# An S4D convolution beside a GLU: spectra at 2048 quarter-shifted frequencies instead of 2049 whole ones

## The chip, the cores and the metric

The kernel runs on one core of one Trainium2 chip. The metric is device time in microseconds (us) of one execution. Engines are named as in the profile: PE (TensorE matmul) and PEld (its weight loads), DVE (VectorE), ACT (ScalarE), POOL (GpSimd), and SP, which here only issues DMAs. SP, ACT and POOL each have a DMA queue; an instruction that waits in such a queue holds all that is behind it on the same engine.

## What is computed

A token sequence of 2048 x 448 is layer-normed, and two branches read the result: an S4D convolution and a gated linear unit (GLU). Cut to what matters:

```python
def _A_ref(u, log_A_real, A_imag, C_real, C_imag, log_dt, D_skip):   # L = 2048, D = 448, N = 256
    dt = exp(log_dt); A = -exp(log_A_real) + 1j * A_imag; C = (C_real + 1j * C_imag) * dt[:, None]
    P = exp((A * dt[:, None])[:, :, None] * arange(L)[None, None, :])
    K = 2.0 * einsum("dn,dnl->dl", C, P).real
    y = irfft(rfft(u_t, 2 * L) * rfft(K, 2 * L), 2 * L)[:, :, :L]     # causal convolution
    return y + u * D_skip
def _B_ref(x, w_gate, w_up, w_down):                                  # F = 1792
    return (sigmoid(x @ w_gate) * (x @ w_up)) @ w_down
xn = layernorm(A_u)
return A_u + _A_ref(xn, ...) + _B_ref(xn, ...)
```

## The kernel before

Two Python generators write the program: `conv()` (norm, the kernel K, the spectra) and `glu()`. A planner loop at the end of the kernel function takes the next piece from the generator whose planned share done, `done[i] / total[i]`, is smaller; a piece tells its planned cost when it yields. `total[0]` is the sum of the convolution's planned costs, its last term `17 * WS` with `WS = 4.5`. The tile framework then orders each engine's instructions, with priorities (`hp`) and `issue_after` hints, and each engine runs its list in order. When the GLU comes to its last output tiles it yields `None`, and the convolution is written out to its end before the GLU goes on.

**The kernel stage** (`kgen`): for 56 chunks of 8 channels, DVE makes three products (`Et` twice, lines 591 and 592, `Ft`, line 593) from magnitudes (POOL) and phases (ACT), and PE multiplies them (`ko`, line 605). Every fourth chunk ACT copies `ko` to `ks` (line 618), and the first stage of the kernel's transform (`kp`, `kq`, line 555) writes a bank of the kernel's half-done spectra to DRAM (`sk_d`, 14 banks). GLU pieces lie in between: gate and up matmuls (`gu`, line 697, 11 per weight half), `hf` and `hl` on DVE (708, 715), the down projection (`po`, line 808).

**The spectra stage** (`spectra`): the convolution is done as a transform of 64 x 64 points. `x1_d` holds the first stage of x's transform, `sk_d` that of the kernel's. The channels are in two halves `h` of 224. A step `(h, k)` treats four first-stage frequencies `k` to `k + 3`:

- `loads` issues, on SP, two DMAs of x (`sx`), one of the tables (`tb`), one of the kernel (`skl`), three steps ahead (`NLD = 3`).
- `there` is the second stage for both on PE (`sp`, line 890: 32 matmul records of 128 x 64), a copy of the kernel's spectra by ACT (`kc`, line 898), and the complex product on DVE (lines 901 to 904).
- `back` is the first stage of the way back on PE (`pv`, line 917: 16 records), two ACT copies to `vt` (line 923), and four stores to `v_d` (line 935). It is called in the next step.
- `turned` loads a step's rows of `v_d` into `vp`, a tile with one buffer (line 941). It is called one step after `back`.
- `last(h, m)` is the last stage: 32 products `pv<-vp,wf` (line 952), added to the accumulators by DVE (line 960). After its first two calls for the first half, `out` stores finished tokens through the SP, ACT and POOL queues in turn (line 237).

With whole frequencies 0 to 2048, first-stage frequencies 0 and 32 are each real in part: frequencies 0 to 31 are packed in eight steps for each half, and frequency 32 gets a step of its own for both halves, `(None, 32)`, second of 17. That step uses 64 rows, its own tables `t32`, and the kernel rows of all 14 banks. `last` for the first half runs in the steps `due[0]` and `due[0] + 1`; `due` is set when `turned(0, 28)` is called:

```python
steps[0:2] = [steps[1], (None, 32), steps[0]]
...
if t == (0, 28):
    due = [n + 1]
```

The second half's `turned` calls wait until that last stage is through, since `vp` has one buffer. The last stage of the second half is written by `glu()`, after the final down projections.

Of the kernel before, what the change touches and what calls it, by code (L numbers as in the profile page):

```python
# [11 lines left out]
F32 = mybir.dt.float32  # L12
# [10 lines left out]
F = 1792  # L23
NA = 32
NB = 64
NK1 = 33
TWO_PI = 2.0 * math.pi
MAGIC = 1.5 * 2.0**23
NFT = F // 128
# [26 lines left out]
def _tables():  # L56

    a = np.arange(NA)[:, None]
    k1 = np.arange(NK1)[None, :]
    ang = 2 * np.pi * ((a * k1) % 64) / 64.0  # L60


    wk = np.zeros((4, NA, 2, 2, 32))

    wx = np.zeros((4, NA, 64))
    for j in range(4):
        wk[j, :, 0, j % 2] = np.cos(ang)[:, :32]
        wk[j, :, 1, j % 2] = -np.sin(ang)[:, :32]
        wk[j, :, 1, j % 2, 0] = np.cos(ang)[:, 32]
        wx[j, :, :NK1] = np.cos(ang)  # L70
        wx[j, :, NK1:] = -np.sin(ang)[:, 1:32]
    b = np.arange(NB)[:, None]
    k2 = np.arange(64)[None, :]
    tab = np.zeros((NK1, 128, 128))
    bk = np.zeros((2, 2, 64, 2, 128))
    for q in range(NK1):
        al = 2 * np.pi * ((b * (q + 64 * k2)) % 4096) / 4096.0
        c, s = np.cos(al), np.sin(al)
        tab[q] = np.block([[c, -s], [s, c]])
        if q in (0, 32):  # L80


            for h in range(2):

                split = lambda t: t.reshape(64, 2, 32).transpose(0, 2, 1)
                both = lambda r, i: np.stack([split(r), split(i)], 3).reshape(64, 128)
                bk[q // 32, h, :, 0] = both(c.T, s.T)
                bk[q // 32, h, :, 1] = both(-s.T, c.T)

    tab[0, 64:] = 0.0  # L90
    t32 = np.concatenate([tab[32][:, None], bk[1].reshape(128, 2, 128)], 1)
    tab = tab[:32].reshape(8, 4, 128, 128).transpose(0, 2, 1, 3)

    wf = np.zeros((2, 2, 4, 8, 32, NA))
    for k in range(32):
        ang = 2 * np.pi * ((k * (64 * np.arange(NA)[None] + np.arange(64)[:, None])) % 4096) / 4096.0
        re = (1.0 if k == 0 else 2.0) / 4096.0 * np.cos(ang)
        im = -2.0 / 4096.0 * np.sin(ang)
        if k == 0:
            im = np.broadcast_to(np.cos(np.pi * np.arange(NA))[None] / 4096.0, im.shape)  # L100
        wf[:, 0, k % 4, k // 4] = re.reshape(2, 32, NA)
        wf[:, 1, k % 4, k // 4] = im.reshape(2, 32, NA)
# [13 lines left out]
    return {  # L116
        "c_wk": f(wk, (128, 2, 64)),
        "c_wx": f(wx, (128, 64)),
        "c_tab": f(tab, (8, 128, 4, 128)),
        "c_t32": f(t32, (128, 3, 128)),  # L120
        "c_bk": f(bk[0], (128, 2, 128)),
        "c_wf": f(wf, (128, 32, NA)),
        "c_sel": f(sel, (128, 512)),
        "c_id": np.eye(128, dtype=np.float32),
    }
# [3 lines left out]
def s4d_glu_kernel(ctx, tc, io):  # L129
# [700 lines left out]
    def spectra(pf):  # L830
# [19 lines left out]
        def loads(h, k):  # L850
            sx = pf.tile([128, 4, H], F32, name="sx", bufs=NLD)
            sk = pf.tile([128, 7, 4, 32], F32, name="skl", bufs=NLD)
            if k == 32:

                nc.sync.dma_start(sx[:64, 0:2].rearrange("b h d -> b (h d)"), x1_d[32])
                for i in range(2):
                    nc.sync.dma_start(sk[:64, :, i], sk_d[64:, 7 * i : 7 * i + 7, 0])
                return t32, sk, sx
            ds, gs = slice(H * h, H * h + H), slice(7 * h, 7 * h + 7)
            nc.sync.dma_start(sx[0:64], x1_d[k : k + 4, :, ds].rearrange("k b d -> b k d"))  # L860
# [10 lines left out]
        def after():  # L871
            return tc.issue_after(sp_mm[0].ins)

        def there(k, tb, sk, sx):

            kk, np_ = (64, 64) if k == 32 else (128, 128)
            ys_ = []
            for j in range(2):

                ks = [(0, j, 0)] if k == 32 else [(2 * j + i, 2 * j + i, i) for i in range(2)]  # L880
                pss = []
                for src in (sk, sx):
                    ps = bank("sp")
                    with after():
                        for c in range(2):
                            for t, n, i in ks:
                                to, rhs = ps[64 * i : 64 * i + 64, c], sx[:kk, n]
                                if src is sk:
                                    to, rhs = to.rearrange("p (g d) -> p g d", d=32), sk[:kk, :, n]
                                mm = nc.tensor.matmul(  # L890
                                    to, tb[:kk, t, 64 * c : 64 * c + 64], rhs, start=True, stop=True,
                                    skip_group_check=True,
                                )
                    sp_mm[:] = [mm]
                    pss.append(ps)
                    if src is sk:
                        kc = work("kc", [128, 2, H], 3)
                        nc.scalar.copy(kc[:np_], ps[:np_])
                yy, pd = work("yy", [128, 2, H], 4), work("pd", [128, 2, H], 2)
                xt = pss[1]  # L900
                v.tensor_tensor(yy[:np_], kc[:np_], xt[:np_], ALU.mult)
                v.tensor_tensor(pd[:np_], kc[:np_], xt[:np_, ::-1], ALU.mult)
                v.tensor_tensor(yy[:np_, 0], yy[:np_, 0], yy[:np_, 1], ALU.subtract)
                v.tensor_tensor(yy[:np_, 1], pd[:np_, 0], pd[:np_, 1], ALU.add)
                ys_.append(yy)
            return ys_

        def back(h, k, ys_):
            vt = work("vt", [128, 2, 2, H], 2)
            bt, n = (t32[:, 1:3], 1) if k == 32 else (bk, 2)  # L910
            pvs = [bank("pv") for _ in range(n)]
            with after():
                for j in range(2):
                    for e in range(2):
                        for i in range(n):
                            s = slice(64 * i, 64 * i + 64)
                            mm = nc.tensor.matmul(  # L917
                                pvs[i][:, j], bt[s, e], ys_[j][s, e], start=(e == 0), stop=(e == 1),
                                skip_group_check=True,
                            )  # L920
            sp_mm[:] = [mm]
            for i in range(n):
                nc.scalar.copy(vt[:, i], pvs[i])


            for j in range(2):
                for i in range(n):
# [48 lines left out]
        for n, (h, k) in enumerate(steps):  # L976

            sp_mm[:] = glu_mm
            if prev is not None:
                back(*prev)  # L980
            cur = there(k, *ld[n])
            if n + NLD < len(steps):
                ld.append(loads(*steps[n + NLD]))
            if 4 <= n < 8:
# [159 lines left out]
```

## Time and profile before

| | us |
|---|---|
| three timed runs | 740.15, 739.62, 736.60 (median 739.62) |
| the profiled execution | 742.26, span 740.5 |
| PE busy | 683.2 (92% of the span) |
| DVE, ACT, POOL busy | 562.3, 421.7, 376.8 |
| mean granted TensorE clock | 0.967 of full speed |
| kernel stage: first and last `kp` products | about 178 to 552 |
| spectra stage: first `sp` to last `pv` of `back` | 557.6 to 717 |

Rows of the profile read: start, duration, engine, line, operation, output <- inputs, count, and in brackets how long the engine was idle before and what released it. Groups give total busy time, mean ns of one, the idle time before, and its releasers. In the chain, a row is a stretch of the path that ended last. Matmuls overlap, so their single durations add up to more than their stretch; the chain's stretches don't overlap. A record count for fp32 matmuls is twice that of the matmuls in the code.

### The profile page before, as it was taken

How to read it: one execution, taken by the hardware profiler on the slowest of the kernel's cores; microseconds unless marked ns; L12 is line 12 of the kernel's file. 1: busy time of each engine (PE TensorE's matmuls, PEld its weight loads, DVE VectorE, ACT ScalarE, POOL GpSimd, SP SyncE). 2: the span in 40 equal slices, each digit the busy share in tenths (PEclk: the TensorE clock that was granted, in tenths of full speed). 3: DMA queues.
4: the chain of work that ended last, by engine and by line, in shares of the span. 5: the costliest groups of instructions: out<-in, count | busy, mean ns of one | idle time of the engine just before them, and what ended most of it. 6: DMA issues, size and time to landing. Idle time of an engine off the chain costs nothing.

```text
span 740.5 us, 19082 instructions
## 1 busy us (share of the span) xinstructions
PE 683.2 (92%) x7780; PEld 537.0 (73%) x7780; DVE 562.3 (76%) x776; ACT 421.7 (57%) x650; POOL 376.8 (51%) x423
## 2 busy tenths in 40 slices
PE   2797899997999999889989999999999999998994
PEld 1675688785887787556767887888877777776783
DVE  5679997699889989878569978987865555554553
ACT  3535445667688877887567867866742222322310
POOL 2111018697678987964538685796855002341001
PEclk9898899997999999979999999999999999999997
DMA  9936428524413452625852243232169999999646
GB/s 207 219 84 182 119 79 245 173 88 160 165 50 108 163 191 80 183 82 151 267 190 91 79 131 114 96 104 70 59 154 282 255 245 239 234 242 258 173 132 163
DMA packets 93287, 116.76 MB, mean 158 GB/s; under 512 B 12176, under 2 KB 81168, under 8 KB 92944
## 3 DMA queue, kind: packets, MB, share of 16 engines
q1 hardware_dynamic: 83888, 95.08, 46.4%
q10 hardware_dynamic: 6736, 14.57, 6.2%
q0 software_dynamic: 2576, 5.90, 3.2%
q8 instruction: 61, 1.00, 0.6%
q14 instruction: 26, 0.21, 0.1%
HBM read 70.75 MB, written 44.76 MB: 156 GB/s over the span
## 4 chain that ended last, share of the span: by engine, by line
PE 56%; DVE 11%; POOL 9%; ACT 7%; DMA 7%; issue 4%; SPq 3%; ACTq 1%; POOLq 0%; DVEq 0%
PE gu L697 21%; PE po L808 14%; PE sp L890 7%; PE ko L605 5%; PE pv L917 4%; POOL me L507 4%; PE tr L529 3%; POOL mf L507 3%; DVE Ft L593 1%; DVE Et L591 1%; POOL dl L778 1%; ACT S L540 1%; DMA acc_d<-acc 1%; DVE Et L592 1%; DVE wl L752 1%
## 5 line engine op out<-in xcount | busy, mean ns | idle before, releaser
L507 POOL TENSOR_TENSOR me<-me,pm 128x32 f32<-128x32 f32 (+1 forms) x168 | 143.2, 852 | 87.8 <-DVE Et L592 76.0
L507 POOL TENSOR_TENSOR mf<-mf,pm 128x64 f32<-128x64 f32 (+1 forms) x112 | 123.0, 1099 | 4.2
L697 PE MATMUL gu<-xh,wh 128*128 128x512 f32 x336 | 101.8, 409 | 4.2 <-ACT xh L218 4.2
L591 DVE TENSOR_TENSOR Et<-me,S 128x1024 f32<-128x1024 f32 x56 | 84.6, 1511 | 17.2 <-ACT S L540 15.9
L697 PE MATMUL gu<-xh,wl 128*128 128x512 f32 x336 | 96.9, 396 | 0.0
L697 PE MATMUL gu<-xl,wh 128*128 128x512 f32 x336 | 96.7, 393 | 0.0
L808 PE MATMUL po<-dh,hh 128*128 128x448 f32 x224 | 86.3, 385 | 5.2 <-DVE acc L813 2.5
L592 DVE TENSOR_TENSOR Et<-me,S 128x1024 f32<-128x1024 f32 x56 | 78.7, 1405 | 10.8 <-ACT me L520 10.3
L808 PE MATMUL po<-dl,hh 128*128 128x448 f32 x224 | 84.2, 376 | 1.1 <-POOL dl L778 1.1
L808 PE MATMUL po<-dh,hl 128*128 128x448 f32 x224 | 83.1, 373 | 0.0
L593 DVE TENSOR_TENSOR Ft<-mf,S 128x1024 f32<-128x1024 f32 x56 | 78.5, 1402 | 6.0 <-POOL mf L507 3.1
L537 ACT ACTIVATE S<-tr 128x1024 f32<-128x1024 f32 x56 | 57.6, 1029 | 41.0 <-PE tr L529 38.3
L697 PEld LDWEIGHTS gu<-xh,wh 128*128 128x128 f32 x336 | 62.2, 192 | 23.4 <-ACT xh L218 5.8
L713 ACT CAST hh<-hf 128x512 fp32r<-128x512 f32 x56 | 35.0, 625 | 74.8 <-DVE hf L708 58.4
L605 PEld LDWEIGHTS ko<-Et,Ft 128*32 128x32 f32 x3584 | 55.0, 111 | 30.6 <-issue 11.9
L697 PEld LDWEIGHTS gu<-xh,wl 128*128 128x128 f32 x336 | 64.4, 192 | 15.5 <-DVE pl L306 0.7
L605 PE MATMUL ko<-Et,Ft 128*32 128x64 f32 x3584 | 65.7, 224 | 10.7 <-DVE Ft L593 7.6
L697 PEld LDWEIGHTS gu<-xl,wh 128*128 128x128 f32 x336 | 63.5, 189 | 14.2 <-issue 0.7
L708 DVE SCALAR_TENSOR_TENSOR hf<-th,gu 128x512 f32<-128x512 f32 x56 | 38.2, 682 | 37.1 <-PE gu L697 28.3
L540 ACT ACTIVATE S<-S,hpi 128x1024 f32<-128x1024 f32 x56 | 65.5, 1170 | 0.0
L813 DVE SCALAR_TENSOR_TENSOR acc<-po,acc 128x448 f32<-128x448 f32 x80 | 48.3, 616 | 20.6 <-PE po L808 20.5
L715 DVE TENSOR_TENSOR hl<-hf,hh 128x512 fp32r<-128x512 f32 x56 | 47.6, 851 | 16.6 <-ACT hh L713 16.6
(196 smaller groups left out, 1286.7 us busy)
## 6 DMA issues: line engine op xcount, KB each, us to landing
sk_d<-sk ACTq DMA_DIRECT2D x14, 512.0 KB
sx<-x_d SPq DMA_DIRECT2D x32, 224.0 KB
skl<-sk_d SPq DMA_DIRECT2D x16, 448.0 KB
vp<-v_d SPq DMA_DIRECT2D x16, 448.0 KB
v_d<-vt SPq DMA_DIRECT2D x62, 112.0 KB
wt_d<-wh SPq DMA_DIRECT2D x9, 512.0 KB
wt_d<-wl SPq DMA_DIRECT2D x9, 512.0 KB
wl<-wt_d SPq DMA_DIRECT2D x9, 512.0 KB
```

Of the source, the lines that this page charges most:

```text
L507: ins = nc.gpsimd.tensor_tensor(m[:, :, w + a : 2 * w : n], m[:, :, a:w:n], par(base + i).unsqueeze(2).to_broadcast([128, 4 * DC, w // n]) ...
L537: nc.scalar.activation(rows(cs), pv, AF.Abs)
L540: sins[:] = [nc.scalar.activation(cs, cs, AF.Sin, scale=-TWO_PI, bias=hpi)]
L591: v.tensor_tensor(Et[:, :, :, 32:64], two(me[:, :, 32:64]), S[:, 1::-1], ALU.mult)
L592: v.tensor_tensor(Et[:, :, :, 0:32], two(me[:, :, 0:32]), S[:, 1:3, :, ::-1], ALU.mult)
L593: fts[:] = [v.tensor_tensor(Ft, two(mf), S[:, 3:5], ALU.mult)]
L605: mm = nc.tensor.matmul(ko[32 * j : 32 * j + 32, sl], Ft[:, cc, DC * h + 4 * q + j], Et[:, cc, DC * h + 4 * q + j], start=(k == 0), stop=( ...
L697: glu_mm[:] = [nc.tensor.matmul(ps, a_, b_, start=(n == 0), stop=(n == len(mm) - 1))]
L715: v.tensor_tensor(hl, hf, hh, ALU.subtract)
L808: glu_mm[:] = [nc.tensor.matmul(po, a_[:, bs], w_, start=(n == 0), stop=(n == 3 * fc - 1))]
L813: v.scalar_tensor_tensor(acc[:, b], po, 0.5, acc[:, b], ALU.mult, ALU.add)
L890: mm = nc.tensor.matmul(to, tb[:kk, t, 64 * c : 64 * c + 64], rhs, start=True, stop=True, skip_group_check=True,)
```

## The change

The 4096-point transforms at frequencies 0 to 2048 are replaced by transforms at the 2048 frequencies 4q + 1 over 8192: each is shifted by a quarter of a step, none is real, and a 32 x 64 set holds all that is needed. So `NK1` is 32 instead of 33; the tables are built for the new angles; `t32`, its DMA, the branch for step 32 in `loads`, `there` and `back`, and the store of step 0 by every second row are gone. There are 16 steps, in their natural order, the first being `(0, 0)`. In `back` every step uses the same table `bk`. The first half's `turned(0, 28)` now comes at step 9 (it was step 10), and `due = [n + 2]`, so that `last(0, ...)` still runs in steps 11 and 12. `total[0]` has `16 * WS`: 480 instead of 484.5, which changes the planner's interleaving of both generators from some place on. Cut to its core:

```diff
-NK1 = 33
+NK1 = 32
...
-    ang = 2 * np.pi * ((a * k1) % 64) / 64.0
+    ang = 2 * np.pi * ((a * (4 * k1 + 1)) % 128) / 128.0
...
-        al = 2 * np.pi * ((b * (q + 64 * k2)) % 4096) / 4096.0
+        al = 2 * np.pi * ((b * (4 * q + 1 + 128 * k2)) % 8192) / 8192.0
...
-        t32 = pg.tile([128, 3, 128], F32, name="t32", tag="rd", bufs=RB)
...
-            if k == 32:
-
-                nc.sync.dma_start(sx[:64, 0:2].rearrange("b h d -> b (h d)"), x1_d[32])
-                for i in range(2):
-                    nc.sync.dma_start(sk[:64, :, i], sk_d[64:, 7 * i : 7 * i + 7, 0])
-                return t32, sk, sx
...
-                ks = [(0, j, 0)] if k == 32 else [(2 * j + i, 2 * j + i, i) for i in range(2)]
...
-            bt, n = (t32[:, 1:3], 1) if k == 32 else (bk, 2)
...
-                    if k == 32:
-                        to, fr = v_d[j, 32::64], vt[0:128:2, 0, j]
-                    elif k1 == 0:
-                        to, fr = v_d[h, 0::64], vt[0:128:2, i, j]
-                    else:
-                        to, fr = v_d[h, 8 * (k1 % 4) + k1 // 4 :: 32], vt[:, i, j]
-                    nc.sync.dma_start(to.rearrange("r w d -> w r d"), fr)
+                    to = v_d[h, 8 * (k1 % 4) + k1 // 4 :: 32]
+                    nc.sync.dma_start(to.rearrange("r w d -> w r d"), vt[:, i, j])
...
-        nc.sync.dma_start(t32, io["c_t32"])
...
-        steps[0:2] = [steps[1], (None, 32), steps[0]]
...
-            if prev is not None and prev[1] < 32:
+            if prev is not None:
                 wait.append(prev[:2])
...
                 if t == (0, 28):
-                    due = [n + 1]
+                    due = [n + 2]
...
-    total = [sum(Y0) + 11 * WP + 8 * WX + 14 + NCK * WK + HOLE + 17 * WS, 2 * (4 + NFT * 14.8) - HELD]
+    total = [sum(Y0) + 11 * WP + 8 * WX + 14 + NCK * WK + HOLE + 16 * WS, 2 * (4 + NFT * 14.8) - HELD]
```

Changed line numbers do not matter below: rows of the profile of before carry the lines of before.

More of the change, by code (lines that the diff above doesn't have):

```diff
@@ L72, in _tables @@
-    b = np.arange(NB)[:, None]
+        wk[j, :, 0, j % 2] = wx[j, :, 0] = np.cos(ang)
+        wk[j, :, 1, j % 2] = wx[j, :, 1] = -np.sin(ang)
     k2 = np.arange(64)[None, :]
     tab = np.zeros((NK1, 128, 128))
-    bk = np.zeros((2, 2, 64, 2, 128))
     for q in range(NK1):
-        al = 2 * np.pi * ((b * (q + 64 * k2)) % 4096) / 4096.0
+        al = 2 * np.pi * ((b * (4 * q + 1 + 128 * k2)) % 8192) / 8192.0
         c, s = np.cos(al), np.sin(al)
         tab[q] = np.block([[c, -s], [s, c]])
[L80 to L88, printed above, removed]
@@ L90, in _tables @@
-    tab[0, 64:] = 0.0
-    t32 = np.concatenate([tab[32][:, None], bk[1].reshape(128, 2, 128)], 1)
-    tab = tab[:32].reshape(8, 4, 128, 128).transpose(0, 2, 1, 3)
-    wf = np.zeros((2, 2, 4, 8, 32, NA))
[L95 to L102, printed above, removed]
+    tab = tab.reshape(8, 4, 128, 128).transpose(0, 2, 1, 3)
@@ new lines, in _tables @@
+    al = 2 * np.pi * ((b * k2) % 64) / 64.0
+    split = lambda t: t.reshape(64, 2, 32).transpose(0, 2, 1)
+    both = lambda r, i: np.stack([split(r), split(i)], 3).reshape(64, 128)
+    bk = np.zeros((2, 64, 2, 128))
+    bk[:, :, 0] = both(np.cos(al).T, np.sin(al).T)
+    bk[:, :, 1] = both(-np.sin(al).T, np.cos(al).T)
+    wf = np.zeros((2, 2, 4, 8, 32, NA))
+    l = 64 * np.arange(NA)[None] + np.arange(64)[:, None]
+    for k in range(NK1):
+        al = 2 * np.pi * (((4 * k + 1) * l) % 8192) / 8192.0
+        wf[:, 0, k % 4, k // 4] = (np.cos(al) / L).reshape(2, 32, NA)
+        wf[:, 1, k % 4, k // 4] = (-np.sin(al) / L).reshape(2, 32, NA)
@@ L119, in _tables @@
         "c_tab": f(tab, (8, 128, 4, 128)),
[L120 to L121 removed]
+        "c_bk": f(bk, (128, 2, 128)),
         "c_wf": f(wf, (128, 32, NA)),
@@ L885, in there @@
                         for c in range(2):
[L886 to L887 removed]
+                            for i in range(2):
+                                n = 2 * j + i
+                                to, rhs = ps[64 * i : 64 * i + 64, c], sx[:, n]
                                 if src is sk:
[L889 removed]
+                                    to, rhs = to.rearrange("p (g d) -> p g d", d=32), sk[:, :, n]
                                 mm = nc.tensor.matmul(
[L891 removed]
+                                    to, tb[:, n, 64 * c : 64 * c + 64], rhs, start=True, stop=True,
                                     skip_group_check=True,
@@ L897, in there @@
                         kc = work("kc", [128, 2, H], 3)
-                        nc.scalar.copy(kc[:np_], ps[:np_])
+                        nc.scalar.copy(kc, ps)
                 yy, pd = work("yy", [128, 2, H], 4), work("pd", [128, 2, H], 2)
                 xt = pss[1]
[L901 to L904, printed above, removed]
+                v.tensor_tensor(yy, kc, xt, ALU.mult)
+                v.tensor_tensor(pd, kc, xt[:, ::-1], ALU.mult)
+                v.tensor_tensor(yy[:, 0], yy[:, 0], yy[:, 1], ALU.subtract)
+                v.tensor_tensor(yy[:, 1], pd[:, 0], pd[:, 1], ALU.add)
                 ys_.append(yy)
@@ L909, in back @@
             vt = work("vt", [128, 2, 2, H], 2)
-            bt, n = (t32[:, 1:3], 1) if k == 32 else (bk, 2)
-            pvs = [bank("pv") for _ in range(n)]
+            pvs = [bank("pv") for _ in range(2)]
             with after():
@@ L914, in back @@
                     for e in range(2):
-                        for i in range(n):
+                        for i in range(2):
                             s = slice(64 * i, 64 * i + 64)
                             mm = nc.tensor.matmul(
-                                pvs[i][:, j], bt[s, e], ys_[j][s, e], start=(e == 0), stop=(e == 1),
+                                pvs[i][:, j], bk[s, e], ys_[j][s, e], start=(e == 0), stop=(e == 1),
                                 skip_group_check=True,
@@ L980, in spectra @@
                 back(*prev)
-            cur = there(k, *ld[n])
+            cur = there(*ld[n])
             if n + NLD < len(steps):
```

17 lines of the change are left out of this document (6 added, 11 removed).

## The prediction

> **What bounds the kernel now.** I read the page's busy shares and chain first, then the stretches, then the waits of TensorE (PE).
>
> ```profile
> span 740.5 us, 19082 instructions
> PE 683.2 (92%) x7780; PEld 537.0 (73%) x7780; DVE 562.3 (76%) x776; ACT 421.7 (57%) x650; POOL 376.8 (51%) x423
> PE 56%; DVE 11%; POOL 9%; ACT 7%; DMA 7%; issue 4%; SPq 3%; ACTq 1%; POOLq 0%; DVEq 0%
> ```
>
> PE is busy for 92% of the span and carries over half of the chain; no other engine comes near. What matters is where its missing 57 us lie. The stretches (us from the start; then busy PE, PEld, DVE, ACT and POOL; granted clock; DMA share; GB/s) give it by stage:
>
> ```profile
> 190.00:552.00 362.00, 347.78 (x5304) 276.84 (x5306) 308.12 (x326) 268.82 (x394) 260.19 (x283) 0.99 0.40 126
> 540.00:560.00 20.00, 19.32 (x336) 15.38 (x336) 10.82 (x12) 8.93 (x15) 10.50 (x15) 1.00 0.60 161
> 560.00:580.00 20.00, 20.00 (x122) 14.69 (x119) 12.63 (x24) 5.91 (x11) 6.23 (x7) 1.00 1.09 312
> 660.00:680.00 20.00, 17.87 (x185) 12.66 (x174) 11.77 (x23) 2.94 (x6) 6.76 (x7) 1.00 0.97 267
> ```
>
> From 560 us on, in the spectra stage that the change edits, PE has no gap except one of 20.00 - 17.87 = 2.1 us after 660, at full clock. DMA is saturated there too (share about 1), yet no load is late for PE, since each is issued three steps ahead. In the kernel stage, 190 to 552 us, PE is idle for 362.00 - 347.78 = 14.2 us, in short waits for DVE above all:
>
> ```profile
> PE ko L605 <- DVE Ft L593: 7.2, 9, 1.4
> PE ko L605 <- DVE Et L591: 1.9, 2, 1.2
> ```
>
> So an instruction taken from PE in the spectra stage shortens the kernel by its own time; one moved in the kernel stage counts by what it does to PE's waits for DVE.
>
> **The change, part by part.** The profiled execution took 742.26 us, 1.76 more than its span; the three timed runs have a median of 739.62, which is 2.64 less. I make the sum against 742.26 and carry the difference over.
>
> *The step that goes.* Step 32's products and the steps around it, from the chain:
>
> ```profile
> 567.77 3.17 PE sp L890 x16
> 573.66 1.71 PE pv L917 x8
> 575.36 3.18 PE sp L890 x32
> 583.76 1.71 PE pv L917 x16
> ```
>
> Step 32 has half the matmul records of a full step and costs the same, 3.17 + 1.71 = 4.9 us, all on the chain with no idle beside it. Its one DVE pass, ACT copies and stores run beside PE; nothing is late next for want of them. Term: -4.9. The Trainium skill, TensorEngine Tiling (Array Packing), Key Properties, says that tiles work independently and in parallel; if the step's 64-row products had packed at that rate, half of it, 2.4, would be the saving. The rows show no packing (16 records in 3.17, 32 in 3.18), and they decide.
>
> *Loads.* In before, SP sits on step 32's kernel spectra, which need the last bank of the kernel stage; the third step's loads queue behind it:
>
> ```profile
> 540.78 17.60 SPq L857 DMA_DIRECT2D skl<-sk_d  x2
> ```
>
> In the changed kernel's SP queue, the first three steps' loads stand in a row, with no wait for that bank. A full step brings 2 x 224 KB of x spectra, 448 KB of kernel spectra and a 256 KB table. That work moves into 540 to 558, where DMA is 0.60 busy. It buys no PE time (the first products stand behind the same gate matmuls), but keeps DMA from falling behind: PE gains 4.9 us, and DMA only the light step's 0.64 MB (from the shapes: 192 KB of tables, 224 of loads, 224 of stores), 2.4 us at the 267 GB/s of the last stretch above. Term: 0; if that cover failed, +2.5.
>
> *The last stage of the first half.* Its load is issued at step 9, not 10, its products stay at step 11.
>
> ```profile
> 650.48 0.51 SPq L941 DMA_DIRECT2D vp<-v_d  x1
> 658.97 2.72 PE L952 MATMUL pv<-vp,wf 64*32 64x224 f32 x64
> ```
>
> The load has 8.5 us in before, and the products show no idle ahead of them. A step more buys nothing: 0. If they stayed one step behind, it would be the same 8.5.
>
> *The stores behind that stage.* The 2.1 us at 660 come from ACT: three stores of its queue (the first row) wait for older DMAs, the third for the x load that SP issued at 663.60. The two copies that free PE's banks stand behind them.
>
> ```profile
> 665.25 4.01 ACTq L237 DMA_DIRECT2D out_dram<-ac  x3
> 663.60 1.40 SPq L860 DMA_DIRECT2D sx<-x_d  x1
> 670.89 0.98 PE L890 MATMUL sp<-skl,tb 128*64 128x224 f32 x8 [0.61 <-ACT vt L923]
> 675.75 0.96 PE L952 MATMUL pv<-vp,wf 64*32 64x224 f32 x16 [1.47 <-DVE pd L902]
> ```
>
> In the changed order the stores still stand behind step 11's copies, and still wait for that step's x load. PE has 11 gate matmuls between, not 22, so 2.6 us less cover, but the extra 11 now lie ahead of step 11, which gives the lagging DMA 2.6 us more. One activation no longer stands behind the stores. If the load lands as late after step 11 as now, PE waits 4.1 instead of 2.1; if 4 us sooner, not at all. Ends -2.1 and +2.0; I take 0, as the two shifts of 2.6 cancel.
>
> *The planner's order.* The convolution's planned total falls from 484.5 to 480, so each of its pieces counts for more and the GLU's pieces come a little earlier against it. The first difference on PE lies at 174 us:
>
> ```profile
> 173.05 0.86 PE L697 MATMUL gu<-xl,wh 128*128 128x512 f32 x3
> 177.68 0.36 PE L555 MATMUL kp<-wk,ks 64*64 64x64 f32 x1 [3.77 <-ACT ks L618]
> 180.83 1.94 PE L605 MATMUL ko<-Et,Ft 128*32 128x64 f32 x64 [1.19 <-DVE Et L591]
> 179.47 1.21 DVE L591 TENSOR_TENSOR Et<-me,S 128x1024 f32<-128x1024 f32 x1
> 180.61 0.68 DVE L708 SCALAR_TENSOR_TENSOR hf<-th,gu 128x512 f32<-128x512 f32 x1
> ```
>
> PE idles 3.77 for the copy of ks, then 1.19 for Et. The changed queue has 14 gate matmuls ahead, not 3: 11 more at 0.238 (the gate row below) fill 2.6 of the 3.77. But only 9 first-stage products follow, not 29, and on DVE the 0.68 of hf stands ahead of that Et, so the second wait grows from 1.2 to about 3.1. Idle 4.4 instead of 5.0: -0.6. The clock falls in this place:
>
> ```profile
> 175.00:180.00 5.00, 1.96 (x58) 1.78 (x58) 4.88 (x6) 5.00 (x10) 4.69 (x5) 0.66 0.68 224
> 180.00:185.00 5.00, 4.17 (x74) 3.17 (x75) 5.00 (x6) 3.38 (x5) 2.75 (x2) 0.50 0.25 81
> 325.00:330.00 5.00, 5.00 (x15) 2.13 (x15) 4.71 (x7) 4.43 (x9) 2.59 (x5) 0.50 0.41 91
> 322.98 1.60 PE L605 MATMUL ko<-Et,Ft 128*32 128x64 f32 x64 [1.34 <-DVE Ft L593]
> ```
>
> If it stayed up, the products, transforms and 11 gate matmuls after 180.83 would take about 2.5 us less (ko 1.94 for 1.10, for one); so the ends are 0 and -2.5 beside the -0.6. The Trainium skill, TensorE: Matmul & The Clock Gate, HAM oscillation, says that PE should have no idle gap over about 3.4 us to keep its clock: by it the changed gaps, 1.2 and 3.1, would save the 2.5. But at 325 the clock is 0.50 after no wait over 1.34, so gaps alone don't decide it here, and I take 0.
>
> For the rest, to 552 us, I laid both kernels' queues side by side: for each of the 56 products PE's queued work since the last one, and DVE's, by these rows (gate, down projection, product; DVE's three for a product and two for a gate; the number before the idle is the mean in ns) and the groups' means for the others.
>
> ```profile
> 552.44 5.23 PE gu L697 x22
> 717.03 9.31 PE po L808 x45
> 542.12 1.03 PE ko L605 x64
> L591 DVE TENSOR_TENSOR Et<-me,S 128x1024 f32<-128x1024 f32 x56 | 84.6, 1511 | 17.2 <-ACT S L540 15.9
> L592 DVE TENSOR_TENSOR Et<-me,S 128x1024 f32<-128x1024 f32 x56 | 78.7, 1405 | 10.8 <-ACT me L520 10.3
> L593 DVE TENSOR_TENSOR Ft<-mf,S 128x1024 f32<-128x1024 f32 x56 | 78.5, 1402 | 6.0 <-POOL mf L507 3.1
> L708 DVE SCALAR_TENSOR_TENSOR hf<-th,gu 128x512 f32<-128x512 f32 x56 | 38.2, 682 | 37.1 <-PE gu L697 28.3
> L715 DVE TENSOR_TENSOR hl<-hf,hh 128x512 fp32r<-128x512 f32 x56 | 47.6, 851 | 16.6 <-ACT hh L713 16.6
> ```
>
> Taken one product at a time, DVE's work exceeds PE's by 46 us in all before and 55 after (the sum of the positive excesses); taken four at a time, by 18.8 and 18.0. Scaling the 14.2 us of idle by these gives +2.7 and -0.6; I take +1.0, between. One place stands out: over products 21 to 28 PE has 43.5 us queued against DVE's 51.1 before, and 37.1 against 51.0 after, 6.3 shorter, most of which is moved to the four products behind.
>
> *Sum.* -4.9 + 0 + 0 + 0 - 0.6 + 1.0 = -4.5: 737.8 against the profiled 742.26, and 739.62 - 4.5 = 735.1 against the median.
>
> **Rivals.** *The gaps close.* The clock stays up at 174 (-2.5) or the stores let ACT go early (-2.1): one of them gives about 732.8, both 730.5. For it: both waits sit on a coincidence that the new order breaks. Against: the clock at 325, and DMA as full as before.
>
> *The order gives the saving back.* Single products count: +2.7 instead of +1.0, and the stores cost +1.0: 735.1 + 2.7 = 737.8, no change that can be told. About 0.5%, 3.7 us, is what a measurement of this kernel can tell from none. For it: the three DVE rows add up to 4.3 us a product, beside 1.5 for hf and hl of each gate, so DVE has little to spare.
>
> *Slower: products 21 to 28.* PE there waits for DVE the whole 6.3 us longer, DVE then idles behind the 33 gate matmuls queued in one piece after, and the clock, which falls at 322 to 335 now, stays at half for one more such stretch, about 5.1 us (10 us at half speed). That is -5.5 without my +1.0, then +11.4: 745.5. It decides from about 9.2 us of added waits, where it makes up 5.5 and 3.7. For it: PE's idle in 300 to 325 and the clock's fall behind it are there already, in this place. Against: the four products behind hold 4.1 us more PE work, in which DVE can get ahead.
>
> *DMA becomes the bound.* If the early loads wait for space and not for the bank, PE waits the 2.5 at an early step: 737.6. Against: three steps of prefetch.
>
> **How the numbers follow.** The forecast gets 0.38, its own range being 733 to 737: two thirds below 735.9 (faster by over 0.5%), 0.25, the rest within, 0.13. The gaps closing: 0.18, faster. The saving given back: 0.17, same. DMA: 0.05, same. Slower: 0.22. Together 0.43, 0.35 and 0.22. The range reaches from both gaps closed and the order's -0.6 (730.5 - 1.6, 728.9, less 1 for the runs' spread, which was 736.6 to 740.15) to the slower case at 745.5: 728 to 746.
>
> **What would show it.** Right: in the chain after the kernel stage, the step of 16 and 8 records is gone and the steps are 3.2 and 1.7 as before; PE's gaps after 560 sum to about 2; SP has no 17-us entry; idle from 190 to the end of the products is 14 to 17. Wrong: a new wait of PE for sp or pv at steps 1 to 3 (loads), a hold of ACT over 6 us at the stores, or idle over 9 us with a clock of 0.5 between products 21 and 28, which would lead to the slower case.

## The result, and the profile after

The changed kernel takes 744.1 us (median of 17 runs, 738.9 to 755.05) against 739.12 for the kernel before (17 runs, 734.01 to 743.3): ratio 1.0074, 95% interval 1.005 to 1.0097. It is slower by 0.7%; the forecast was 735.1, faster by 0.6%.

The first profiled execution of the changed kernel, at 755.05, was a disturbed one, of a kind that the ratios leave out, so the rows below are of another execution of the same kernel (run e1 of the experiments), which took 745.06. Lines of the changed kernel are 17 to 33 lower than those of before (`ko` 605 is 588, `Ft` 593 is 576, `sp` 890 is 864, `pv` 917 is 890, `vt` 923 is 896).

The page of the changed kernel: span, busy time and the chain's shares.

```profile
span 743.2 us, 18994 instructions
PE 686.2 (92%) x7756; PEld 537.7 (72%) x7756; DVE 566.1 (76%) x768; ACT 419.4 (56%) x647; POOL 374.1 (50%) x423
PE 60%; DVE 11%; DMA 9%; POOL 8%; issue 5%; ACT 3%; SPq 3%; POOLq 0%; DVEq 0%; ACTq 0%
```

PE still bounds the kernel. It executes 24 records fewer and yet is busy for 3 us longer; in the chain DMA has 9% where it had 7%. The stretches (columns as in the prediction) show where:

```profile
175.00:180.00 5.00, 3.81 (x94) 3.02 (x98) 5.00 (x5) 3.85 (x6) 3.11 (x2) 0.50 0.31 98
190.00:560.00 370.00, 354.42 (x5230) 280.01 (x5232) 310.62 (x322) 264.56 (x390) 253.86 (x281) 0.96 0.40 122
240.00:250.00 10.00, 6.67 (x76) 5.54 (x77) 8.53 (x8) 9.80 (x16) 6.74 (x7) 0.66 0.64 234
515.00:540.00 25.00, 20.74 (x325) 17.44 (x324) 23.66 (x20) 13.30 (x20) 12.26 (x16) 0.93 0.13 42
560.00:580.00 20.00, 16.93 (x129) 12.69 (x121) 5.78 (x12) 5.62 (x11) 10.33 (x12) 0.84 0.90 256
```

In the kernel stage PE idles about as long as before (370.00 - 354.42 = 15.6 us, 14.2 before), but half of it is gathered in two places, 240 to 250 (3.3 us) and 515 to 540 (4.3 us), and in both the clock falls, to 0.66 and 0.93. The kernel before had no gap in either, at full clock:

```profile
240.00:250.00 10.00, 10.00 (x129) 8.12 (x121) 10.00 (x8) 9.22 (x15) 9.77 (x9) 1.00 0.54 196
515.00:540.00 25.00, 25.00 (x411) 21.04 (x410) 21.78 (x23) 17.08 (x25) 18.66 (x18) 1.00 0.21 61
```

The mean clock of the stage is 0.96, where before had 0.99 up to 552. A third place lies at 560 to 580, where before had no gap: 3.1 us, clock 0.84.

*The first place, 239 to 245 us.* Rows of the timelines of SP, ACT, DVE and PE there:

```profile
227.46 0.43 SPq L614 DMA_DIRECT2D wraw<-in_B_w_up_dram  x1
234.07 0.34 SPq L752 DMA_DIRECT2D dt_d<-dl  x1
234.45 1.13 SPq L616 DMA_DIRECT2D wraw<-in_B_w_up_dram  x2
238.60 1.05 ACT L731 CAST wh<-wraw 128x1024 fp32r<-128x1024 f32 x1 [4.70 <-DMA wraw<-in_B_w_up_dram]
239.69 1.85 DVE L735 TENSOR_TENSOR wl<-wraw,wh 128x1024 fp32r<-128x1024 f32 x1 [2.83 <-ACT wh L731]
243.32 1.93 PE L588 MATMUL ko<-Et,Ft 128*32 128x64 f32 x64 [3.46 <-DVE Ft L576]
```

Read upwards: PE waits 3.46 us for `Ft`; `Ft` stands on DVE behind `wl` of a GLU weight (`w_up`); `wl` waits for ACT's cast; the cast waits 4.70 us for the load of that weight; and the last two DMAs of the load stand on SP behind a store of `dl`, which goes out at 234.07. The GLU piece that needs this weight has moved ahead in the new order: its `wl` stands one product earlier in DVE's list than before.

*The second place, 519 to 530 us.* Rows of the timelines of POOL and DVE, then PE's waits between 515 and 540:

```profile
519.02 2.40 POOL L743 TENSOR_TENSOR wl<-wraw,wh 128x1024 fp32r<-128x1024 f32 x1
527.92 1.05 POOL L490 TENSOR_TENSOR me<-me,pm 128x512 f32<-128x512 f32 x1
519.23 3.27 DVE L576 TENSOR_TENSOR Ft<-mf,S 128x1024 f32<-128x1024 f32 x1
524.42 5.63 DVE L576 TENSOR_TENSOR Ft<-mf,S 128x1024 f32<-128x1024 f32 x1 [0.79 <-POOL mf L490]
```

```profile
PE po L791 <- DVE acc L796: 2.0, 1, 2.0
PE ko L588 <- DVE Ft L576: 1.4, 1, 1.4
PE ko L588 <- DVE Et L574: 0.8, 1, 0.8
```

An `Ft` pass took 1.21 us at the shortest before, 1.40 in the mean, and at most 2.09. Here two take 3.27 and 5.63. The first ends at 522.50, which is 1.08 us after POOL's `wl` ends (521.42); the second ends at 530.05, again 1.08 us after the last of POOL's magnitudes ends (528.97), the last of a series of products without a gap. Neither pass reads what POOL wrote last (`wl` and `me`), so it is not data that they wait for: in both, DVE does its work only when POOL is through. That is not so everywhere. Of the 168 passes of the three kinds, 126 ran beside a product of POOL in the kernel before, and none took over 2.18 us; in the changed kernel, between 508 and 514 us, passes of 1.5 to 1.65 us lie beside POOL products drawn out to 1.9 and 2.05, so there the two engines take turns. What makes 519 to 530 different was not tried. PE pays 4.3 us in the three waits. The group of all 56 passes shows the sum (changed kernel):

```profile
L576 DVE TENSOR_TENSOR Ft<-mf,S 128x1024 f32<-128x1024 f32 x56 | 85.2, 1522 | 12.7 <-ACT S L523 5.9
```

It was 78.5 us, 1402 each: 6.7 us more, of which the two passes are 2.1 + 4.4 = 6.5.

*The third place, 566 to 580 us*, from the chain of waits:

```profile
566.50 8.04 DMA bk<-in_c_bk_dram
574.68 3.36 PE pv L890 x16
578.03 4.46 PE sp L864 x32
587.70 1.72 PE pv L890 x16
589.42 3.18 PE sp L864 x32
```

The step of 16 and 8 records is gone, and full steps cost 1.72 + 3.18 as before. But the first `back` waits for its table `bk`, which POOL issues at 566.50, 8 us ahead of the landing (PE's own wait is 3.07 us). Before, POOL issued it at 553.69; now the loads of a GLU weight stand ahead of it in POOL's queue.

### The profile page after: what moved, and what is told of

It is laid out like the page before. It is cut to its first block, busy times and chain, and to the rows that moved or that the text cites. A ratio compares the mean times of both kernels' runs of the same rounds, so it can differ in the third digit from the quotient of the medians.

```text
span 753.3 us, 18994 instructions
## 1 busy us (share of the span) xinstructions
PE 685.1 (91%) x7756; PEld 536.6 (71%) x7756; DVE 562.9 (75%) x768; ACT 419.0 (56%) x647; POOL 371.2 (49%) x423
## 4 chain that ended last, share of the span: by engine, by line
PE 35%; DMA 9%; DVE 3%; POOL 3%; issue 3%; ACT 2%; ACTq 1%; SPq 1%; POOLq 0%; DVEq 0%
PE gu L680 13%; PE po L791 7%; PE sp L864 5%; PE ko L588 3%; PE pv L890 3%; PE tr L512 2%; DVE Ft L576 1%; DMA v_d<-vt 1%; DMA sx<-x_d 1%; DMA acc_d<-acc 1%; DMA skl<-sk_d 1%; DMA bk<-in_c_bk_dram 1%; ACTq L665 1%; DMA out_dram<-ac 1%; POOL wl L743 1%
## 5 line engine op out<-in xcount | busy, mean ns | idle before, releaser
L490 POOL TENSOR_TENSOR me<-me,pm 128x32 f32<-128x32 f32 (+1 forms) x168 | 139.7, 832 | 94.0 <-DVE Et L575 82.1
L576 DVE TENSOR_TENSOR Ft<-mf,S 128x1024 f32<-128x1024 f32 x56 | 87.5, 1562 | 13.8 <-ACT S L523 6.1
L575 DVE TENSOR_TENSOR Et<-me,S 128x1024 f32<-128x1024 f32 x56 | 76.9, 1373 | 15.4 <-ACT me L503 12.4
L574 DVE TENSOR_TENSOR Et<-me,S 128x1024 f32<-128x1024 f32 x56 | 78.2, 1396 | 8.8 <-ACT S L523 8.3
L680 PEld LDWEIGHTS gu<-xh,wl 128*128 128x128 f32 x336 | 63.8, 190 | 15.3 <-DVE pl L289 0.7
L698 DVE TENSOR_TENSOR hl<-hf,hh 128x512 fp32r<-128x512 f32 x56 | 50.8, 907 | 25.1 <-ACT hh L696 25.1
```

Source lines behind the costliest of these rows:

```text
L490: ins = nc.gpsimd.tensor_tensor(m[:, :, w + a : 2 * w : n], m[:, :, a:w:n], par(base + i).unsqueeze(2).to_broadcast([128, 4 * DC, w // n]) ...
L574: v.tensor_tensor(Et[:, :, :, 32:64], two(me[:, :, 32:64]), S[:, 1::-1], ALU.mult)
L575: v.tensor_tensor(Et[:, :, :, 0:32], two(me[:, :, 0:32]), S[:, 1:3, :, ::-1], ALU.mult)
L576: fts[:] = [v.tensor_tensor(Ft, two(mf), S[:, 3:5], ALU.mult)]
L680: glu_mm[:] = [nc.tensor.matmul(ps, a_, b_, start=(n == 0), stop=(n == len(mm) - 1))]
L698: v.tensor_tensor(hl, hf, hh, ALU.subtract)
```

## The experiments

All ratios are against the kernel before, on the same chip in the same session; an empty row stands between sessions, each of which was on another chip. Of these sessions only the first has the changed kernel itself.

| run | what | ratio, 95% interval |
|---|---|---|
| e1_after | the changed kernel | 1.0111 (1.0057 to 1.0166) |
| e2_after_plan17 | planner's total of before, 484.5 | 0.9939 (0.9902 to 0.9976) |
| e3_before_plan16 | kernel before with total 480 | 1.0126 (1.0068 to 1.0184) |
| e4_after_noact | changed, stores off ACT's queue | 1.0011 (0.9976 to 1.0045) |
| | | |
| e5_no_last_series | changed, without POOL's last series (the last two products use old magnitudes) | 1.0040 (1.0008 to 1.0071) |
| e6_early_load | changed, weight load earlier | 1.0079 (1.0044 to 1.0113) |
| e7_three | both, and `bk` in its own place | 0.9988 (0.9963 to 1.0012) |
| e8_plan17_three | the same three, total 484.5 | 0.9972 (0.9944 to 1.0000) |
| | | |
| e9_bk_own | changed, `bk` in its own place | 1.0114 (1.0066 to 1.0163) |
| e10_plan17_stores | 484.5, stores off ACT, early load, `bk` | 0.9939 (0.9915 to 0.9963) |
| e11_plan17_due1 | 484.5, last stage one step behind | 1.0004 (0.9976 to 1.0032) |
| e12_total489 | changed, total 489 | 1.0068 (1.0045 to 1.0092) |
| | | |
| e13_three_stores | e7 (so without the last series) and stores off ACT | 0.9876 (0.9840 to 0.9912) |
| e14_due1_stores | e11 and stores off ACT | 0.9898 (0.9881 to 0.9915) |
| e15_before_stores | kernel before, stores off ACT | 0.9965 (0.9941 to 0.9988) |

**The two parts of the change, apart.** e1 is the changed kernel as it is.

> The changed kernel as it is, once more with a profile, since the first profiled execution was a slow one. Order theory (the planner's total of 480 spoils the kernel stage): idle of PE from 190 us to the last ko product is 22 to 28 us, against 14.2 before. Stores theory (ACT held behind the first half's stores): PE waits for vt at step 12 by 4 us or more, and for nothing else of that size. DMA theory (the spectra stage is bound by DMA, so the step taken out of PE brings nothing): waits for DMA or for vt all along the stage, and a late vp load at the end. Time 744 by all three.

No theory's signs came as named: idle from 190 us is 15.6 and not 22 to 28, PE never waits for `vt`, and from the spectra stage on it waits for DMAs only twice, 3.1 us for `bk` and 1.3 for a `vp` at the end.

e2 keeps the new transform and gives the planner its old total; PE's, DVE's and ACT's queues then equal those of before up to the spectra stage, POOL's altogether.

```diff
-NCK * WK + HOLE + 16 * WS
+NCK * WK + HOLE + 17 * WS
```

> The changed kernel with the planner's total of before, 484.5: the instruction queues of PE, DVE, ACT and POOL are then those of before up to the spectra stage; step 32 is still gone. Order theory: 735, about 4 to 5 under before. Stores theory: 742 to 744, as the stores still stand in ACT's queue. DMA theory: 739 to 744, no faster than before.

e3 does the reverse, `16 * WS` in the kernel before.

> The kernel before, with step 32, but the planner's total of 480: its queues are those of the changed kernel up to the spectra stage. Order theory: 747 to 750, before plus what the order costs (about 9). Stores theory: 739 to 742. DMA theory: 739.

Measured: -0.61% for the transform alone, 4.5 us of 739.97; +1.26% for the total alone, 9.3 us. Together 4.8 us or 0.65%, beside the 0.74% (17 runs) and 1.11% (6 runs) of the whole change. So by these runs the step was worth about what the sum said, and the order cost about twice that. The sizes are loose: e2's twelve runs lie between 730.36 and 746.44, and the median of them all is 737.51, 2.5 us under the kernel before. The profile of e3 has the same two `Ft` passes (3.27 us at 518.92, 5.63 us at 524.11) in a kernel that still has its 17 steps.

**The stores on ACT's queue.** e4 moves the first half's stores that ACT issues to SP; PE's, DVE's and POOL's queues stay.

```diff
-out(ac[:, 4 * q : 4 * q + 4], 4 * q, h)
+out(ac[:, 4 * q : 4 * q + 4], 4 * q, h, (nc.sync, nc.scalar if h else nc.sync, nc.gpsimd))
```

> The changed kernel, but the first half's output stores that went through ACT's queue go through SP's; the queues of PE, DVE and POOL are unchanged. Order theory: 742 to 744. Stores theory: 738 to 740, and no wait of PE for vt at step 12. DMA theory: 743 to 744, the wait only moves to another place.

Measured: 1.0 percentage points less than e1, 7 us, though e1's own profile has no wait of PE for `vt`. With both intervals it may be anything from about 0.4 to 1.6 points. I come back to this below.

**The three places.** Each has an edit that leaves the lists of the other engines alone. e5 leaves out POOL's last series, so that nothing runs beside the `Ft` pass at 524:

```diff
 def magnitudes(b):
+    if 2 * b + 2 == NCK: return mes[b % 2], tl[f"mf{b % 2}"]
```

> The changed kernel, with POOL's last series of magnitudes left out (11 POOL instructions, those for the last two products, which then use old magnitudes); the instruction lists of PE, DVE, ACT and SP are the same. In the changed kernel that series runs beside the Ft pass at 524 us, which then takes 5.63 us instead of 1.21, and POOL's wl beside the one at 519 takes it to 3.27; PE waits 4.3 us in three waits behind them. Theory A (the new order costs by a few named waits): the Ft passes near 524 fall to 1.3 or less, and the time falls by 2.5 to 6 us against the changed kernel's 747.8 of the last comparison, ratio to the kernel before 1.003 to 1.008. Theory B (the loss is spread over the order: DVE's excess product by product, and a wait that goes comes back at the next product): the Ft passes shorten, PE waits about as long a little later, ratio 1.009 or more. Theory C (the clock falls by its own timetable): only the waits themselves go, clock loss stays at 15 to 17 us.

PE's waits of e5 between 505 and 540, and from DVE's timeline the `Ft` pass that took 5.63 us in e1:

```profile
PE ko L588 <- DVE Ft L576: 1.0, 1, 1.0
```

```profile
519.99 1.23 DVE L576 TENSOR_TENSOR Ft<-mf,S 128x1024 f32<-128x1024 f32 x1 [1.22 <-ACT S L523]
```

It takes 1.23 us (the pass before it, beside `wl`, still 2.84), PE's waits are 1.0 us for 4.3, and the ratio is 1.0040: 0.3 to 0.7 points less than the changed kernel's two ratios, which are of other sessions and whose intervals overlap with this one. So the wait is shown to go, its price is not measured by this run alone. The wait doesn't come back at the next products, as the second theory had it.

e6 moves the load of the weight ahead on SP and nothing else:

```diff
-raws.append((w_load(f + 1), None))
+with hp(HP) if f == 11 else nullcontext(): raws.append((w_load(f + 1), None))
```

> The changed kernel, with the load of gate weight 12 ahead in SP's list: its last two DMAs stand before the phase loads and the store of dl that waits for POOL, not behind them; nothing else moves on any engine. In the changed kernel ACT waits 4.70 us for that load at 234 to 239 us, DVE 2.83 for ACT's cast, PE 3.46 for Ft at 243. Theory A: these three waits fall below 1 us each, and the time falls by 2 to 4.5 us, ratio 1.005 to 1.009 where the changed kernel had 1.011. Theory B: PE's wait at 243 falls, but as much comes back by 270 us; ratio 1.010 or more.

```profile
227.84 2.19 SPq L616 DMA_DIRECT2D wraw<-in_B_w_up_dram  x2
234.19 1.03 ACT L731 CAST wh<-wraw 128x1024 fp32r<-128x1024 f32 x1
240.27 1.10 PE L588 MATMUL ko<-Et,Ft 128*32 128x64 f32 x64
```

All three waits of that place are gone (SP, ACT and PE timelines of e6): the DMAs go out 6.6 us earlier, and the product starts at 240.27 with no wait, not at 243.32, and takes 1.10 us, not 1.93, as the clock has not fallen. The ratio, 1.0079, is not told apart from that of the changed kernel by itself (its intervals reach from 1.005 to 1.0166).

e7 has both, and `bk` in a tile of its own, loaded by SP ahead of the first steps; e8 is the control with total 484.5.

```diff
-bk = const.tile([128, 2, 128], F32, name="bk", tag="wk", bufs=1)
-nc.gpsimd.dma_start(bk, io["c_bk"])
+bk = const.tile([128, 2, 128], F32, name="bk", bufs=1)
+nc.sync.dma_start(bk, io["c_bk"])
```

> The changed kernel with three waits taken away at once: the early load and the series left out of the two runs before, and bk in a place of its own, loaded by SP ahead of the spectra's loads instead of by POOL behind heavy weight loads (PE waits 3.07 us for it at 575). PE's, DVE's and ACT's lists stay the same. Theory A: the three add up, 7 to 11 us less than the changed kernel, ratio 0.997 to 1.002; with the 4.5 us of the step that goes the kernel is then as fast as the one before or faster, and the order of 480 is no worse than that of 484.5 apart from these places. Theory B: under 4 us less, ratio 1.006 or more. If 3 to 7 us, part is the waits and part stays spread.

> The control: the same three edits in the changed kernel with the planner's total of before (484.5), which had 0.9939. There the last series meets no long Ft pass (2.1 us at most), ACT's wait for the load is 0.74 us, and there is no wait for bk. Theory A: at most 1.5 us less, ratio 0.991 to 0.995. If it gains as much as the run before does (5 us or more), the edits pay for the work left out or for the queue, and not for waits that the order of 480 made.

The same stretches in e7:

```profile
240.00:250.00 10.00, 10.00 (x163) 7.99 (x162) 9.72 (x8) 8.94 (x15) 9.53 (x9) 1.00 0.54 188
515.00:540.00 25.00, 24.02 (x288) 19.99 (x286) 19.42 (x22) 18.65 (x27) 8.52 (x11) 1.00 0.42 127
560.00:580.00 20.00, 20.00 (x145) 15.06 (x145) 10.65 (x23) 5.79 (x11) 3.99 (x3) 1.00 1.11 282
```

PE is full or nearly so in all three and the clock stays up. The ratio is 0.9988: 0.9 to 1.2 points are gone, 6.3 to 9.1 us beside the order's 9.3. In the control the same edits gain nothing (0.9972 beside e2's 0.9939 of another session, and above the 0.991 to 0.995 that was expected), so the gain doesn't come from the work that e5 leaves out. Most of what the order costs lies in these places and the clock behind them, not in a spread-out excess. How it divides between waits and clock can be estimated from stretches of 5 us between 190 and 560, taking for each the missing part of the clock times its length:

| | before | e1 | e3 | e7 | e2 |
|---|---|---|---|---|---|
| PE's idle, us | 14.2 | 15.6 | 17.1 | 12.1 | 13.8 |
| what the clock took, us | 5.1 | 13.7 | 15.3 | 5.1 | 10.3 |

The order of 480 adds 1 to 3 us of idle and 9 to 10 of clock; in e7 the clock's part is back where it was. But these are single executions, and the clock varies by itself: e2, whose lists there are those of before, has 10.3 and is not slower for it. So the larger part is the clock's by these profiles, and the exact division stays open.

e9 has `bk`'s own place alone.

> The changed kernel with bk in a place of its own, loaded by SP ahead of the spectra's loads; the order of all else is the same. PE's wait for bk near 575 (3.07 us, 1.6 in another execution) goes. Theory A (the three waits make up the loss; the last series was worth some 0.7% and the early load 0.3% of a whole 1.2%): what is left for bk is 0.1 to 0.4%, ratio 1.007 to 1.010 where the changed kernel had 1.011 and 1.007. Theory B (DMA is behind by as much anyway, and the next load is late instead): a wait for sx, skl or vp of 2 us or more appears within three steps, ratio 1.010 or more.

It gained nothing. The wait for `bk` is gone, but another stands in the profile, further on. Rows of the timelines of ACT's queue, ACT and PE in e9:

```profile
675.45 4.99 ACTq L220 DMA_DIRECT2D out_dram<-ac  x3
680.48 0.62 ACT L696 CAST hh<-hf 128x512 fp32r<-128x512 f32 x1 [13.99 <-DMA out_dram<-ac]
681.59 1.76 PE L864 MATMUL sp<-skl,tb 128*64 128x224 f32 x8 [5.71 <-ACT vt L896]
```

ACT does nothing for 13.99 us, the last 5 of them while its three stores of finished tokens go out one after the other (675.45 to 680.44), and PE waits 5.71 for the copy behind them that frees its bank. e7 has the same row, 6.04 us; e1 none.

**Other orders.** e12 goes to the other side, `18 * WS`, 489.

> The changed kernel with the planner's total at 489, as far above 484.5 as 480 is below. Theory A (what counts is which pieces meet at a few places): it can come out anywhere from 0.992 to 1.010, and the profile names one or two waits over 2 us where it is slow. Rival (a smaller total sends GLU pieces too early, a larger one is better or equal): ratio 0.995 or less, and no Ft pass over 2.2 us.

PE's waits of e12 between 168 and 560:

```profile
PE ko L588 <- DVE Ft L576: 7.1, 3, 3.6
PE tr L512 <- ACT S L522: 7.1, 5, 3.2
PE kp L538 <- ACT ks L601: 3.7, 1, 3.7
```

489 is slow too, with other waits (ACT's `S` among them, and no `Ft` pass over 2.1 us). So 480 is no exception: 484.5 is the best of the three, and nothing in the plan foretells it.

**Last stage and stores.** e11 has total 484.5 and the first half's last stage one step behind its load:

```diff
-due = [n + 2]
+due = [n + 1]
```

> The changed kernel with the planner's total of before, and the first half's last stage one step behind the load of its last rows, not two (due = n + 1): its products come in steps 10 and 11. The prediction gave both the same cover of 8.5 us. If that holds, ratio 0.992 to 0.996, as with two steps; if the load's landing is late by then, PE waits 1 to 6 us for vp at the first product of the stage, ratio 0.996 to 1.003.

Rows of e11 (ACT's queue, ACT, PE):

```profile
656.81 3.83 ACTq L220 DMA_DIRECT2D out_dram<-ac  x3
660.74 0.60 ACT L688 ACTIVATE th<-gu 128x512 f32<-128x512 f32 x1 [14.80 <-DMA out_dram<-ac]
648.57 2.06 PE L919 MATMUL pv<-vp,wf 64*32 64x224 f32 x64 [2.51 <-DMA vp<-v_d]
661.81 1.76 PE L864 MATMUL sp<-skl,tb 128*64 128x224 f32 x8 [5.09 <-ACT vt L896]
```

The load is 2.51 us late and the stores hold PE for 5.09. e10 is the 484.5 order with stores off ACT, early load and `bk`; e13, e14 and e15 take the stores off ACT in e7, in e11 and in the kernel before, with e4's edit.

> The changed kernel with the planner's total of before (484.5), the first half's stores taken from ACT's queue to SP's, the early load of gate weight 12 and bk in its own place; it computes everything. If the stores hold ACT as in the order of 480 (1.0011 where the kernel with them had 1.0111, at the same chip), 0.3 to 1% goes from 0.9939: ratio 0.985 to 0.991. If they cost something only where PE stands still behind them, which the order of 484.5 shows in no profile, it is 0.992 to 0.996.

> The changed kernel (planner's total 480) with the three waits taken away (last series left out, early load, bk in its own place) and the first half's stores moved from ACT's queue to SP's; PE's, DVE's and POOL's lists are those of the run with the three alone (0.9988), in whose profile PE waits 6.0 us for ACT's copy to vt behind those stores. If that hold is the rest of what 480 loses against 484.5 (0.9939): no wait for vt over 1 us, ratio 0.992 to 0.996. If the hold is a coincidence of one execution and the rest is spread over the order: 0.997 to 1.000.

> The changed kernel with total 484.5 and the last stage one step behind its load (1.0004, with PE waits of 5.09 us for vt and 2.46 for vp), with the first half's stores moved from ACT's queue to SP's. If the one step costs through the stores, which with 11 gate matmuls behind them and not 22 reach PE through ACT: the 5.09 goes, the 2.46 may stay, ratio 0.994 to 0.997. If it costs through DMA, being full at that place, a wait of 4 us or more comes back at vp, sx or skl, and the ratio stays at 0.999 to 1.003.

> The kernel before with the first half's stores moved from ACT's queue to SP's; its profile has waits of PE behind them of 0.61 and 1.47 us. If the hold is as large as profiled there, 0.5 to 2 us go: ratio 0.997 to 0.9995. If it varies from execution to execution as in the changed kernel (0 to 6.5 us), up to 3 us on the median: 0.995 to 0.998.

Stretch 660 to 680 in e7, then in e13, whose PE, DVE and POOL lists are the same:

```profile
660.00:680.00 20.00, 13.88 (x144) 9.43 (x145) 9.33 (x20) 2.45 (x5) 3.12 (x4) 0.83 0.95 250
```

```profile
660.00:680.00 20.00, 19.96 (x193) 14.64 (x192) 10.73 (x22) 5.89 (x11) 0.88 (x2) 1.00 0.94 249
```

The 6.1 us of idle are gone and the clock is up from 0.83. e13's 0.9876 is lower than either expectation, and so is e14's 0.9898; why is not known. Within one session the edit gave 1.0 points (e1 to e4) and 0.35 (e15); between sessions 1.1 (e7 to e13, e11 to e14). e10 showed nothing beyond e2, and e2's profile has a wait of 0.40 only. The hold is of the stores, but how much of it reaches PE differs from one execution to the next: in the changed kernel itself it was 6.5 us in the execution of 755.05 and none in that of 745.06 (e1). Over the profiles, PE's longest wait for `vt` was 0 (e1), 0.4 (e2), 0.6 (e3), 1.3 (e5), 2.4 (e6), 2.9 (e12), 3.1 (e8), 5.1 (e11), 5.7 (e9) and 6.0 us (e7), and there is no such wait in the profiles of the four changed kernels with the stores on SP (e4, e10, e13, e14). What sets it was not tried.

With the stores moved, one step behind (e14) is no worse than two: its wait for `vp` is 0.92 us. e14 computes everything and is 1.0% faster than the kernel before, 732.78 against 738.89 us; e10, which computes everything too, is 0.6% faster.

## Why the prediction was wrong

**The step: right, in size as far as the runs tell.** Predicted -4.9, measured -4.5 (interval -7.3 to -1.8) by e2, 2.5 by the median of all its runs. The reading that its 64-row products show no packing was too quick: they all write to the same 64 rows of the bank, so they stand in one tile of PE's array, while those of a full step alternate between two. That fits 32 records in the time of 16.

**The order at 174 us: right.** Predicted waits of 1.2 for `ks` and 3.1 for `Et`; the PE timeline of the changed kernel has

```profile
173.02 0.27 PE L538 MATMUL kp<-wk,ks 64*64 64x64 f32 x1 [1.23 <-ACT ks L601]
176.19 1.94 PE L588 MATMUL ko<-Et,Ft 128*32 128x64 f32 x64 [2.61 <-DVE Et L574]
```

1.23 and 2.61. The clock fell there all the same (0.50 at 175 to 180, above). The Trainium skill, TensorE: Matmul & The Clock Gate, HAM oscillation, asks for no idle gap of PE over about 3.4 us. By that rule these gaps would have left the clock up, which was weighed at 2.5 us. The trace disagrees: both gaps were shorter, and the clock was at half. In e5, whose lists are the same there, only the second gap occurred, and the clock stayed at 1.00:

```profile
175.00:180.00 5.00, 3.67 (x117) 3.01 (x118) 5.00 (x6) 4.05 (x6) 4.92 (x3) 1.00 0.06 17
176.33 1.10 PE L588 MATMUL ko<-Et,Ft 128*32 128x64 f32 x64 [2.30 <-DVE Et L574]
```

So what the clock does here differs between executions of one order.

**The order to 552 us: the step that failed.** I took +1.0 with ends -0.6 and +2.7, all of it as added idle of PE. e3 puts the whole order at +9.3 (interval 5.0 to 13.6). The idle itself came out as foreseen, 15.6 us, inside the 14 to 17 that I had named as a sign of being right. What the sum had at nothing is what the clock takes when the idle gathers (13.7 us in e1 for 5.1 before, by the estimate above) and the wait for `bk` behind this stage. Three things were wrong in it. First, only PE's and DVE's work was laid side by side, so what DVE itself waits for was missing: at product 14 it waits for a load that is queued on SP behind a store. Second, DVE's work was counted by group means of before, 1402 ns for `Ft`, as if a pass cost the same wherever it falls; beside POOL's series it cost 5.63. Third, I scaled the idle of before, while idle gathered in one place also brings the clock down. Products 21 to 28, the place singled out, were not it: PE's waits from 300 to 350 are 3.4 us in e1, where the slower rival needed over 9 in added waits. That rival was near the right time by luck, 745.5 for 744.1: it named the wrong place.

**Loads: the cover held, though not as I had it.** No load of `sx`, `tb` or `skl` was late. But SP's queue did not run free: in the changed kernel the second step's `tb` goes out only at 558.31 and its `skl` at 564.54. The profile puts the first of these waits, 11.3 us, down to a store of `sk_d`, so the loads are held even without step 32; whether by the bank or for room is not shown. And `bk`, which POOL issues, was not looked at. Its wait of 1.3 to 3.1 us stands in the profiles of the changed kernel and of e4, e5 and e6, yet taking it away alone (e9) changed no time that could be told.

**Last stage: wrong, without weight in the sum.** I said that one step behind would have the same cover, 8.5 us. e11 shows a late `vp` (2.51) and 5.09 behind the stores, 1.0004 for e2's 0.9939 (different sessions, the intervals touch). e14, where the stores are moved, has 0.9898: it was the stores more than the cover of the load that made it dear.

**Stores: mis-sized.** Taken at 0 with ends -2.1 and +2.0. The hold reaches 6.5 us in single executions, and in the order of 480 it costs 7 us in all (e1 to e4), against 2.6 in the kernel before (e15).

## What to carry to other kernels

A planned total that feeds an interleaving is not a side effect of a change but a second change: one kernel with 480, 484.5 and 489 came out at 1.0111, 0.9939 and 1.0068, the last in another session, a spread larger than the step it was adjusted for, so try the edit with the old constant first. When two orders are compared on paper, follow the waits of the engine that feeds the bottleneck one level down (its loads, and POOL beside it), and don't price an instruction by a group's mean where another engine can hold it up. Keep stores of results off the queue of an engine whose copies free the bottleneck's banks.

## What was not expected of the hardware

Two DVE passes with two operands in SBUF did next to no work while POOL ran its products, and one of them not only for one instruction: the 5.63 us pass ended 1.08 us after a whole unbroken series, and such a pass takes 1.21 by itself. The Trainium skill, SBUF — State Buffer, SBUF: two separate sides, says that a DVE instruction with two SBUF inputs and a GpSimd one that reads SBUF contend for a shared pair of ports, and that the one that starts first holds it for its whole instruction while the other blocks fully. The trace agrees that it blocks fully, and here the hold lasted over several instructions, the longest of which took 1.05 us. It is the exception: apart from that pass and the one of 3.27 us, the passes beside POOL took 2.18 us at most.

The granted clock fell behind waits of PE of 3.46 us (0.66 over 240 to 250) and 6.04 us (0.83 over 660 to 680), and did not fall in the same places once the waits were gone (e7, e13). Length alone does not decide: it also fell behind waits of 1.23 and 2.61 us (e1 at 175), and stayed at 1.00 behind one of 2.91 (e12, 660 to 690). So a wait can cost more than its length.
